# Attention, MoE and MoE on one core: k and v products on two column halves of TensorE, their copies and the norm's small addition on ScalarE

## The chip, the cores and the metric

The kernel runs on one core of a Trainium2 chip. The metric is the device time of one execution in microseconds (us). The engines are called by the profile's names: PE is TensorE (PEld is its weight load), DVE is VectorE, ACT is ScalarE, POOL is GpSimd, SP issues the DMAs.

## The reference

Three layers follow each other. Cut to what matters:

```python
kv = einsum('bhsd,bhse->bhde', k, v)            # 4 batches, 8 heads, 576 tokens, 64 channels, float32
o  = einsum('bhsd,bhde->bhse', q, kv)
x  = o / sqrt(mean(o * o, axis=-1) + 1e-6) * g_norm     # mean over a head's 64 channels
x  = x reshaped to [2304 tokens, 512]
y  = ((x @ w_a) * (x @ w_b)) @ w_out            # weights float64, 512 -> 1536 -> 512
h  = y @ w_in                                   # 512 -> 1024
ln = layernorm(h * softmax(h)) * g_ln
out = ln @ w_out2                               # 1024 -> 512
```

## The kernel before, in words

**Attention.** The 8 heads of a batch are taken as 4 pairs. For a pair, k and v lie beside each other as [128 rows of the sequence, two heads x 64 channels], in four chunks of 128 rows and a tail of 64. `att_kv` (L455) forms k^T v of both heads at once: four matmuls of 128x128 and one of 64x128 for the tail, summed in one PSUM tile `pkv`. Only the two 64x64 blocks on the diagonal are wanted; two DVE copies (L475, L476) put them into `bd`, a 128x128 tile that holds zeros elsewhere. `att_1` (L484) multiplies q by the four `bd` tiles for 128 tokens (the fifth tile of a batch has 64), giving `o` in PSUM. Its norm is a chain through the engines: ACT squares (`sq`, L515) and copies `o` to `x` (L507), DVE sums each head (`r`, L517), DVE multiplies by 1/64 and adds 1e-6 (L519, 8 numbers in a row), POOL raises to the power -1/2 (L521), DVE scales `x` (L522). `att_2` (L527) transposes `x` on PE (`t`, L533) and splits it into `xh` (ACT, L546) and `xl` (DVE, L547). The PSUM tiles pkv, o and t share two slots in turn: a tile waits until the readers of the one two places before it are done.

**Weights.** They come as float64 bits in chunks `raw`; ACT and five DVE instructions (L289 to L307, tiles u and f) decode a chunk, ACT rounds it (L365), POOL makes the low part in two instructions (L366, L367). `w1_0` is the first chunk of feature group 1; `wh` and `wl` are its high and low part.

**The main line.** The first MoE runs over feature groups of 128 and blocks of 384 tokens: `ab` (24 matmuls a block and group, 12 with each of two chunks), and `y` (12). For groups 0 and 1 the six blocks run while attention is still being made; the other groups and the second MoE follow.

**What sets the order.** Every engine takes its instructions in program order. A planner (class `Order`, and the loop from L858) writes that order out, from hand-set durations: PE's order is decided step by step between main line and attention, and the other engines' instructions are placed when their input is expected. So a changed duration or engine in a chain moves instructions on all engines. The planner's price for an `att_kv` block stands at L447, L478 and L852 (1.09).

Of the kernel before, what the change touches and what calls it, by code (L numbers as in the profile page):

```python
# [13 lines left out]
AF = mybir.ActivationFunctionType  # L14
ALU = mybir.AluOpType
AX = mybir.AxisListType

P = 128
# [3 lines left out]
NP = H // 2          # head pairs = k tiles of the model dimension  # L22
# [4 lines left out]
NB = 384             # tokens of a block  # L27
# [3 lines left out]
SC = 4               # whole 128-row chunks of a sequence; the rest is 64 rows  # L31
CH = 512             # columns of a weight chunk

# A float64's upper word, read as a float32, is ordered like its magnitude: from 2^-126 on, where
# the float32s have their full precision, up to the largest value that rounds to a finite float32r.
# [9 lines left out]
class Order:  # L45
    """The order of the instructions: the tensor engine's is decided as it goes, and every other
    engine's operations are issued when what they read is expected to be there."""
# [6 lines left out]
    def chain(self, ops, rank=0, t=None):  # L54
        """Operations (engine, duration, function), each after the one before. Of those that wait
        for an engine the one of the lowest rank goes first, and then the oldest."""
        self.seq += 1
        heapq.heappush(self.events, (self.now if t is None else t, rank, self.seq, 0, list(ops)))

    def until(self, t):  # L60
        """Issue what is due by t."""
# [21 lines left out]
    def wait(self):  # L83
        """Let the next event pass."""
        assert self.events, "nothing left that anything could wait for"
        self.now = max(self.now, self.events[0][0])
        self.until(self.now)

    def load(self, nbytes):
        """A load issued now: when it has arrived."""  # L90
# [4 lines left out]
class Ring:  # L95
    """A rotating buffer's slots: the next one is free once its last user is."""
# [17 lines left out]
def attention_moe_moe_kernel(ctx: ExitStack, tc, kv_in, kv_tail, q_in, g_norm, w1, w_in, w_out2, g_ln, out):  # L114
    """Float32 products are split exactly: hi = the value rounded to float32r (12 bits of
    significand), lo = value - hi (the other 12); hi*hi + hi*lo + lo*hi in three passes.
    The float64 weights come as their bits and become such pairs on the chip."""
# [18 lines left out]
    # Tiles of two banks of PSUM: slot -> when it is free. The attention's two make a fourth.  # L136
# [18 lines left out]
    # ---- constants  # L155
# [20 lines left out]
    # ---- loads: attention's and the weights' chunks ([128, 512] float64s), each kind in its order  # L176
    R_KV, R_TAIL, R_Q, R_RAW = Ring(3), Ring(2), Ring(6), Ring(3)
    arrived = {}                  # what -> (ring slot, tile, when)
# [17 lines left out]
    # Weights between them: so many chunks before the attention's nth load.  # L196
# [4 lines left out]
    def load_one(k):  # L201
# [6 lines left out]
        elif what == "q":  # L208
            r, t, src, n = R_Q, att.tile([P, S], F32, tag="q", name=nm, bufs=6), q_in[x, y], 2304
            if x == 0:  # L210
                # The first block's tokens; the others come later.
# [16 lines left out]
    def loads():  # L228
        """Issue every load whose buffer is free."""
# [21 lines left out]
    # ---- decoding of the weights  # L251
# [10 lines left out]
    def decode_more():  # L262
        """Start on the next chunk, if it is there and the buffers are free."""
# [7 lines left out]
    def rank_of(k):  # L271
        """A chunk's among the attention's tiles: the first ones are wanted soon."""
        return {("w", 0, 0): 1.5, ("w", 0, 1): 1.5, ("w", 0, 2): 2.5, ("w", 1, 0): 2.5}.get(k, 5)

    def decode(k):
# [8 lines left out]
        def a():  # L284
            # |upper word|, on its way to a clamped exponent.
# [10 lines left out]
        def b3():  # L296
            # The float32 of the sign, the exponent and the significand's upper 20 bits.
# [7 lines left out]
        def b5():  # L305
            # The lower 32 bits' value.
# [18 lines left out]
    def store(k, f, u, su, sf, t):  # L325
        """The pair of a chunk, once it has a place."""
# [53 lines left out]
    def wc_used(k):  # L380
        """The last product with a chunk has been issued."""
# [5 lines left out]
    def scale_more():  # L387
        """g_ln goes into the rows of the second MoE's w_out; the first six chunks take the first
        MoE's weights' places, once nothing else wants them."""
# [27 lines left out]
    # ---- attention: the front (k^T v of a pair of heads; q times it for a tile of tokens) and the  # L417
    # back (the transpose of the tile's normalized rows)
# [3 lines left out]
    back = []                      # (ready, b, t, x, ring slot)  # L422
# [21 lines left out]
    def run_front():  # L444
        w, b, i = front.pop(0)
        if w == "kv":
            od.pe(1.09, lambda: att_kv(b, i))  # L447
# [7 lines left out]
    def att_kv(b, p):  # L455
# [3 lines left out]
        o = ps[:, 0:P]  # L459
        for c in range(SC):  # L460
            nc.tensor.matmul(  # L461
                o, lhsT=t[:, c * P:(c + 1) * P], rhs=t[:, (SC + c) * P:(SC + c + 1) * P], start=c == 0, stop=False
            )
        r0 = D * (p % 2)
        nc.tensor.matmul(
            o, lhsT=tl[r0:r0 + D, p // 2, 0:P], rhs=tl[r0:r0 + D, p // 2, P:2 * P], start=False, stop=True
        )
        bd = bds[b % 2, p]

        def done(t):  # L470
# [4 lines left out]
            ("V", 0.13, lambda: nc.vector.tensor_copy(out=bd[0:D, 0:D], in_=ps[0:D, 0:D])),  # L475
            ("V", 0.13, lambda: nc.vector.tensor_copy(out=bd[D:P, D:P], in_=ps[D:P, D:P])),  # L476
            (None, 0, done),
        ], t=od.now + 1.09 + 0.2)  # L478
# [5 lines left out]
    def att_1(b, t):  # L484
        """Attention of 128 (or the last 64) tokens, over the root mean square of each head."""
# [24 lines left out]
        def done(when):  # L510
# [4 lines left out]
            ("A", 0.52, lambda: nc.scalar.activation(out=sq[0:n], in_=o, func=AF.Square)),  # L515
# [3 lines left out]
            ("V", 0.07, lambda: nc.vector.tensor_scalar(  # L519
                out=r[0:n], in0=r[0:n], scalar1=1.0 / D, scalar2=1e-6, op0=ALU.mult, op1=ALU.add)),  # L520
# [472 lines left out]
```

## Time and profile before

| | us |
|---|---|
| runs before | 748.85, 749.93 (median), 753.9 |
| span of the profiled execution | 748.1 |
| PE busy | 726.2 (97%) |
| DVE busy | 483.2 (65%) |
| POOL busy | 281.9 (38%) |
| ACT busy | 237.7 (32%) |

The span runs from the first to the last instruction of the profiled execution; the median run lies 1.8 us above it. Busy shares are means over stages with different limits, so the rows below are read stage by stage. PE records count a float32 matmul twice, since it goes through the array as two records; the main line's float32r matmuls have one record each.

### The profile page before, as it was taken

How to read it: one execution, taken by the hardware profiler on the slowest of the kernel's cores; microseconds unless marked ns; L12 is line 12 of the kernel's file. 1: busy time of each engine (PE TensorE's matmuls, PEld its weight loads, DVE VectorE, ACT ScalarE, POOL GpSimd, SP SyncE). 2: the span in 40 equal slices, each digit the busy share in tenths (PEclk: the TensorE clock that was granted, in tenths of full speed). 3: DMA queues.
4: the chain of work that ended last, by engine and by line, in shares of the span. 5: the costliest groups of instructions: out<-in, count | busy, mean ns of one | idle time of the engine just before them, and what ended most of it. 6: DMA issues, size and time to landing. Idle time of an engine off the chain costs nothing.

```text
span 748.1 us, 10107 instructions
## 1 busy us (share of the span) xinstructions
PE 726.2 (97%) x4024; PEld 680.4 (91%) x4024; DVE 483.2 (65%) x714; ACT 237.7 (32%) x406; POOL 281.9 (38%) x271
## 2 busy tenths in 40 slices
PE   6789999989999999999999999999999999999998
PEld 5668999989999999999999999999878888888887
DVE  4984545489987777777776757566595535546350
ACT  2453435442323232323231313124533222212221
POOL 2774323575746464626262515131421111111110
PEclk9989999999999999999999999999999999999999
DMA  8915230022221212121211110000000000000001
GB/s 291 327 48 172 93 140 1 1 94 76 94 104 50 92 49 93 50 92 47 95 47 67 48 37 29 0 1 1 1 0 29 15 29 28 15 29 14 29 16 55
DMA packets 16334, 46.78 MB, mean 63 GB/s; under 512 B 2080, under 2 KB 3360, under 8 KB 16288
## 3 DMA queue, kind: packets, MB, share of 16 engines
q1 hardware_dynamic: 16288, 46.15, 17.5%
q8 instruction: 31, 0.51, 0.3%
q14 instruction: 15, 0.12, 0.1%
HBM read 41.42 MB, written 4.72 MB: 62 GB/s over the span
## 4 chain that ended last, share of the span: by engine, by line
PE 87%; DVE 8%; issue 1%; DMA 1%; POOL 1%; ACT 1%; SPq 0%; ACTq 0%; POOLq 0%
PE y L643 19%; PE ab L563 12%; PE ab L564 12%; PE ab L565 12%; PE h L565 4%; PE out L565 4%; PE out L564 4%; PE h L563 4%; PE out L563 4%; PE h L564 4%; PE t L792 2%; PE pkv L461 2%; PE o L490 1%; DVE f_w L298 1%; PE t L533 1%
## 5 line engine op out<-in xcount | busy, mean ns | idle before, releaser
L563 PE MATMUL ab<-xh,wh_w 128*128 128x384 f32 x576 | 194.7, 338 | 0.0
L565 PE MATMUL ab<-xh,wl_w 128*128 128x384 f32 x576 | 193.0, 335 | 0.3 <-POOL wl_w L367 0.3
L564 PE MATMUL ab<-xl,wh_w 128*128 128x384 f32 x576 | 192.8, 335 | 0.0
L616 POOL TENSOR_TENSOR gl<-a,gh 128x384 fp32r<-128x384 f32 x72 | 75.8, 1052 | 162.9 <-ACT gh L615 162.9
L656 DVE TENSOR_TENSOR ya<-y,ya 128x768 f32<-128x768 f32 x120 | 111.2, 949 | 6.5 <-PE y L643 5.1
L563 PEld LDWEIGHTS ab<-xh,wh_w 128*128 128x128 f32 x576 | 108.3, 188 | 0.8 <-issue 0.2
L565 PEld LDWEIGHTS ab<-xh,wl_w 128*128 128x128 f32 x576 | 108.4, 188 | 0.6 <-POOL wl_w L367 0.6
L564 PEld LDWEIGHTS ab<-xl,wh_w 128*128 128x128 f32 x576 | 108.4, 188 | 0.0
L643 PE MATMUL y<-gh,wh_w 128*128 128x384 f32 x288 | 98.2, 341 | 1.5 <-ACT gh L615 1.5
L643 PE MATMUL y<-gl,wh_w 128*128 128x384 f32 x288 | 97.3, 338 | 1.4 <-POOL gl L616 1.3
L643 PE MATMUL y<-gh,wl_w 128*128 128x384 f32 x288 | 96.8, 336 | 0.0
L613 DVE TENSOR_TENSOR a<-ab,a 128x384 f32<-128x384 f32 x72 | 39.8, 553 | 80.4 <-ACT a L612 80.2
L366 POOL TENSOR_TENSOR f_w<-f_w,wh_w 128x512 f32<-128x512 f32 x36 | 49.9, 1386 | 64.8 <-ACT wh_w L365 59.6
L612 ACT COPY a<-ab 128x384 f32<-128x384 f32 x72 | 34.4, 478 | 108.5 <-PE ab L565 108.5
L770 DVE TENSOR_REDUCE st<-h 128x1 f32<-128x1024 f32 x18 | 22.0, 1220 | 67.4 <-PE h L565 67.3
L643 PEld LDWEIGHTS y<-gh,wh_w 128*128 128x128 f32 x288 | 54.5, 189 | 2.7 <-ACT gh L615 1.9
L563 PE MATMUL h<-winh,yh 128*128 128x512 f32 x144 | 56.2, 390 | 0.8 <-DVE u L772 0.8
L643 PEld LDWEIGHTS y<-gl,wh_w 128*128 128x128 f32 x288 | 54.6, 190 | 2.2 <-POOL gl L616 2.1
L565 PE MATMUL h<-winh,yl 128*128 128x512 f32 x144 | 56.2, 390 | 0.0
L564 PE MATMUL h<-winl,yh 128*128 128x512 f32 x144 | 56.1, 389 | 0.0
L643 PEld LDWEIGHTS y<-gh,wl_w 128*128 128x128 f32 x288 | 54.6, 190 | 0.0
L615 ACT CAST gh<-a 128x384 fp32r<-128x384 f32 x72 | 36.9, 513 | 47.3 <-DVE a L613 47.1
(92 smaller groups left out, 1168.7 us busy)
## 6 DMA issues: line engine op xcount, KB each, us to landing
raw_w<-in_w SPq DMA_DIRECT2D x36, 512.0 KB, 3.3
kv<-in_kv SPq DMA_DIRECT2D x16, 512.0 KB, 4.8
out<-ot SPq DMA_DIRECT2D x17, 256.0 KB, 2.0
raw_i<-in_w_in SPq DMA_DIRECT2D x8, 512.0 KB, 3.2
raw_o<-in_w_out SPq DMA_DIRECT2D x8, 512.0 KB, 3.2
q<-in_q SPq DMA_DIRECT2D x12, 288.0 KB, 5.6
tail<-in_kv_tail SPq DMA_DIRECT2D x4, 256.0 KB, 5.7
q<-in_q SPq DMA_DIRECT2D x4, 192.0 KB, 4.2
```

What stands on the lines that cost most here:

```text
L366: ("G", 1.23, lambda: nc.gpsimd.tensor_tensor(out=f, in0=f, in1=hi.bitcast(F32), op=ALU.subtract)),
L461: nc.tensor.matmul(o, lhsT=t[:, c * P:(c + 1) * P], rhs=t[:, (SC + c) * P:(SC + c + 1) * P], start=c == 0, stop=False)
L563: nc.tensor.matmul(o, lhsT=ah, rhs=bh, start=first, stop=False)
L564: nc.tensor.matmul(o, lhsT=ah, rhs=bl, start=False, stop=False)
L565: nc.tensor.matmul(o, lhsT=al, rhs=bh, start=False, stop=last)
L612: ("A", 0.41, lambda: nc.scalar.copy(out=a, in_=ps[:, 0, 0:NB])),
L613: ("V", 0.5, lambda: nc.vector.tensor_tensor(out=a, in0=ps[:, 1, 0:NB], in1=a, op=ALU.mult)),
L615: ("A", 0.41, lambda: nc.scalar.copy(out=gh, in_=a)),
L616: ("G", 0.96, lambda: nc.gpsimd.tensor_tensor(out=gl, in0=a, in1=gh.bitcast(F32), op=ALU.subtract)),
L643: nc.tensor.matmul(o, lhsT=x[:, s], rhs=y, start=f == fs[0] and n == 0, stop=f == fs[-1] and n == 2)
L656: op = ("V", 0.87, lambda: nc.vector.tensor_tensor(out=dst, in0=src, in1=dst, op=ALU.add))
L770: ("V", 1.13, lambda: nc.vector.tensor_reduce(out=nmax, in_=ps, axis=AX.XY, op=ALU.max, negate=True)),
```

## The change

The products of a pair are formed head by head: ten matmuls of 64x64 in place of five of 128x128 (the tail included). Head 0 goes to PSUM partitions 0 to 63, head 1 to 64 to 127, so each uses one half of the array's columns, and the two alternate. The two copies to `bd` and the small addition of the norm move from DVE to ACT; the factor 1/64 goes into the square's input scale. The planner's price of an `att_kv` block becomes 0.75, and the ACT copies are planned at 0.25 and the addition at 0.2. Comments are dropped, without effect.

```diff
     def run_front():
...
-            od.pe(1.09, lambda: att_kv(b, i))
+            od.pe(0.75, lambda: att_kv(b, i))
...
     def att_kv(b, p):
...
-        o = ps[:, 0:P]
-        for c in range(SC):
-            nc.tensor.matmul(
-                o, lhsT=t[:, c * P:(c + 1) * P], rhs=t[:, (SC + c) * P:(SC + c + 1) * P], start=c == 0, stop=False
-            )
         r0 = D * (p % 2)
-        nc.tensor.matmul(
-            o, lhsT=tl[r0:r0 + D, p // 2, 0:P], rhs=tl[r0:r0 + D, p // 2, P:2 * P], start=False, stop=True
-        )
+
+        for c in range(SC + 1):
+            for h in range(2):
+                o = ps[h * D:(h + 1) * D, 0:D]
+                if c < SC:
+                    k, v = (t[:, x * P + h * D:x * P + (h + 1) * D] for x in (c, SC + c))
+                else:
+                    k, v = (tl[r0:r0 + D, p // 2, x * P + h * D:x * P + (h + 1) * D] for x in range(2))
+                nc.tensor.matmul(o, lhsT=k, rhs=v, start=c == 0, stop=c == SC)
...
         od.chain([
-            ("V", 0.13, lambda: nc.vector.tensor_copy(out=bd[0:D, 0:D], in_=ps[0:D, 0:D])),
-            ("V", 0.13, lambda: nc.vector.tensor_copy(out=bd[D:P, D:P], in_=ps[D:P, D:P])),
+            ("A", 0.25, lambda: nc.scalar.copy(out=bd[0:D, 0:D], in_=ps[0:D, 0:D])),
+            ("A", 0.25, lambda: nc.scalar.copy(out=bd[D:P, D:P], in_=ps[D:P, 0:D])),
             (None, 0, done),
-        ], t=od.now + 1.09 + 0.2)
+        ], t=od.now + 0.75 + 0.2)
...
-            ("A", 0.52, lambda: nc.scalar.activation(out=sq[0:n], in_=o, func=AF.Square)),
+            ("A", 0.52, lambda: nc.scalar.activation(out=sq[0:n], in_=o, func=AF.Square, scale=D ** -0.5)),
...
-            ("V", 0.07, lambda: nc.vector.tensor_scalar(
-                out=r[0:n], in0=r[0:n], scalar1=1.0 / D, scalar2=1e-6, op0=ALU.mult, op1=ALU.add)),
+            ("A", 0.2, lambda: nc.scalar.activation(out=r[0:n], in_=r[0:n], func=AF.Copy, bias=1e-6)),
...
-                t += 1.32 if w == "t" else 1.09
+                t += 1.32 if w == "t" else 0.75
```

The order changes on all engines at the start, and from batch 3's last `o` on (PE row 456 of 3632 in both) every engine's remaining order is the same in both kernels. Up to that row PE has 324 matmuls of the main line and all 16 `att_kv` blocks in both.

In the names, `r1_3` is batch 1, tile 3; `gl0_0` is group 0, block 0; a last number counts tiles.

POOL where group 1's weights and batch 1's powers are made, before:

```order
L366 TENSOR_TENSOR f_w1_0_353<-f_w1_0_353,wh_w1_0_420 128x512
L616 TENSOR_TENSOR gl0_0_406<-a0_0_404,gh0_0_405 128x384
L367 TENSOR_TENSOR wl_w1_0_421<-f_w1_0_353,u_w1_0_352 128x512
L366 TENSOR_TENSOR f_w1_1_418<-f_w1_1_418,wh_w1_1_456 128x512
L521 TENSOR_TENSOR r1_0_438<-r1_0_438,mhalf_84 128x8
L521 TENSOR_TENSOR r1_1_448<-r1_1_448,mhalf_84 128x8
L521 TENSOR_TENSOR r1_2_473<-r1_2_473,mhalf_84 128x8
L521 TENSOR_TENSOR r1_3_497<-r1_3_497,mhalf_84 128x8
L521 TENSOR_TENSOR r1_4_521<-r1_4_521,mhalf_84 64x8
L367 TENSOR_TENSOR wl_w1_1_457<-f_w1_1_418,u_w1_1_417 128x512
L366 TENSOR_TENSOR f_w1_2_459<-f_w1_2_459,wh_w1_2_560 128x512
```

and now:

```order
L366 TENSOR_TENSOR f_w1_0_353<-f_w1_0_353,wh_w1_0_435 128x512
L367 TENSOR_TENSOR wl_w1_0_436<-f_w1_0_353,u_w1_0_352 128x512
L616 TENSOR_TENSOR gl0_0_448<-a0_0_446,gh0_0_447 128x384
L366 TENSOR_TENSOR f_w1_1_420<-f_w1_1_420,wh_w1_1_486 128x512
L367 TENSOR_TENSOR wl_w1_1_487<-f_w1_1_420,u_w1_1_419 128x512
L521 TENSOR_TENSOR r1_0_481<-r1_0_481,mhalf_84 128x8
L521 TENSOR_TENSOR r1_1_496<-r1_1_496,mhalf_84 128x8
L521 TENSOR_TENSOR r1_2_528<-r1_2_528,mhalf_84 128x8
L521 TENSOR_TENSOR r1_3_544<-r1_3_544,mhalf_84 128x8
L616 TENSOR_TENSOR gl1_0_566<-a1_0_564,gh1_0_565 128x384
L366 TENSOR_TENSOR f_w1_2_485<-f_w1_2_485,wh_w1_2_553 128x512
L367 TENSOR_TENSOR wl_w1_2_554<-f_w1_2_485,u_w1_2_484 128x512
```

The low part of chunk w1_1 moved from behind the five powers of batch 1 to ahead of them, and the fifth power moved behind w1_2.

DVE around the third `xl` of batch 0, on which the first block of the main line waits, before:

```order
L475 COPY bd1_0_94<-pkv1_0_289 64x64
L519 TENSOR_SCALAR r0_3_247<-r0_3_247 128x8
L517 TENSOR_REDUCE r0_4_271<-sq0_4_270 64x8
L476 COPY bd1_0_94<-pkv1_0_289 64x64
L519 TENSOR_SCALAR r0_4_271<-r0_4_271 64x8
L292 TENSOR_SCALAR u_w0_2_190<-u_w0_2_190 128x512
L547 SCALAR_TENSOR_TENSOR xl0_107<-t0_2_311,gn_82,xh0_106 128x4x128
L298 SCALAR_TENSOR_TENSOR f_w0_2_191<-raw_w0_2_146,u_w0_2_190 128x512
L475 COPY bd1_1_96<-pkv1_1_322 64x64
L522 TENSOR_TENSOR x0_3_245<-x0_3_245,r0_3_247 128x512
```

and now:

```order
L522 TENSOR_TENSOR x0_2_249<-x0_2_249,r0_2_251 128x512
L292 TENSOR_SCALAR u_w0_2_218<-u_w0_2_218 128x512
L547 SCALAR_TENSOR_TENSOR xl0_107<-t0_1_294,gn_82,xh0_106 128x4x128
L518 TENSOR_REDUCE r0_4_308<-sq0_4_307 64x8
L298 SCALAR_TENSOR_TENSOR f_w0_2_219<-raw_w0_2_151,u_w0_2_218 128x512
L522 TENSOR_TENSOR x0_3_266<-x0_3_266,r0_3_268 128x512
L547 SCALAR_TENSOR_TENSOR xl0_107<-t0_2_317,gn_82,xh0_106 128x4x128
L303 TENSOR_SCALAR u_w0_2_218<-f_w0_2_219 128x512
L307 SCALAR_TENSOR_TENSOR u_w0_2_218<-raw_w0_2_151,u_w0_2_218 128x512
L289 TENSOR_SCALAR u_w1_0_352<-u_w1_0_352 128x512
```

The copies and L519 are gone, and the scaling of tile 3 (x0_3), which needs the fourth power, now stands ahead of the third `xl`.

PE from the third transpose of batch 0 on, before:

```order
L533 MATMUL t0_2_311<-ident_81,x0_2_230 128x128 x4
L461 MATMUL pkv1_1_322<-kv1_1_184 128x128 x4
L465 MATMUL pkv1_1_322<-tail1_0_173 128x128
L563 MATMUL ab0_0_334<-xh0_106,wh_w0_0_160 128x384
L564 MATMUL ab0_0_334<-xl0_107,wh_w0_0_160 128x384
L565 MATMUL ab0_0_334<-xh0_106,wl_w0_0_161 128x384
L461 MATMUL pkv1_2_340<-kv1_2_198 128x128 x4
L465 MATMUL pkv1_2_340<-tail1_0_173 128x128
```

and now:

```order
L533 MATMUL t0_2_317<-ident_81,x0_2_249 128x128 x4
L468 MATMUL pkv1_0_322<-kv1_0_179 64x64 x8
L468 MATMUL pkv1_0_322<-tail1_0_183 64x64 x2
L563 MATMUL ab0_0_356<-xh0_106,wh_w0_0_166 128x384
L564 MATMUL ab0_0_356<-xl0_107,wh_w0_0_166 128x384
L565 MATMUL ab0_0_356<-xh0_106,wl_w0_0_167 128x384
L533 MATMUL t0_3_361<-ident_81,x0_3_266 128x128 x4
```

A block is eight and two matmuls of 64x64 in place of four and one; the main line now starts behind batch 1's first block (kv1_0) in place of its second, and the fourth transpose comes right behind the first three matmuls.

## Rows read from the trace of the kernel before

**Rows 1.** The page, head: the span.
```profile
span 748.1 us, 10107 instructions
```
**Rows 2.** Busy time of stretches: us, each engine's busy (instructions), PE clock, DMA.
```profile
40.00:60.00 20.00, 15.86 (x98) 13.30 (x98) 18.26 (x34) 9.17 (x17) 17.98 (x12) 0.91 0.32 105
...
16.50:62.30 45.80, 36.47 (x222) 30.82 (x220) 41.36 (x78) 22.55 (x42) 33.90 (x21) 0.93 0.59 208
62.30:131.90 69.60, 69.60 (x448) 66.80 (x447) 32.91 (x67) 30.20 (x53) 22.34 (x17) 1.00 0.23 79
131.90:748.10 616.20, 609.28 (x3305) 573.41 (x3304) 403.39 (x549) 181.82 (x308) 222.11 (x225) 1.00 0.12 43
```
**Rows 3.** PE's waits in 0 to 130: total us, times, longest.
```profile
PE t L533 <- DVE xl L547: 2.6, 5, 1.1
PE t L533 <- DVE r L519: 2.0, 1, 2.0
PE t L533 <- DVE x L522: 2.0, 2, 1.6
```
**Rows 4.** DVE in order of time: start, us, instruction.
```profile
25.54 0.82 DVE L519 TENSOR_SCALAR r<-r 128x8 f32<-128x8 f32 x1
...
32.42 1.14 DVE L289 TENSOR_SCALAR u_w<-u_w 128x512 f32<-128x512 f32 x1
```
**Rows 5.** Instructions on tiles pkv and r: ns min/median/max, first and last start.
```profile
L475 DVE COPY bd<-pkv x16: 203/216/217, 8.2 to 104.6; 64x64 f32<-64x64 f32 x16
L476 DVE COPY bd<-pkv x16: 227/227/229, 8.4 to 104.8; 64x64 f32<-64x64 f32 x16
...
L519 DVE TENSOR_SCALAR r<-r x20: 154/164/833, 17.5 to 133.4; 128x8 f32<-128x8 f32 x16, 64x8 f32<-64x8 f32 x4
L521 POOL TENSOR_TENSOR r<-r,mhalf x20: 1628/1637/2102, 17.8 to 133.6; 128x8 f32<-128x8 f32 x16, 64x8 f32<-64x8 f32 x4
```
**Rows 6.** PE in order of time around two small tiles and one k, v block.
```profile
83.92 1.09 PE L490 MATMUL o<-bd,q 128*64 128x128 f32 x8
...
85.91 0.33 PE L643 MATMUL y<-gh,wl_w 128*128 128x384 f32 x1
86.08 1.05 PE L461 MATMUL pkv<-kv 128*128 128x128 f32 x8
87.07 0.48 PE L465 MATMUL pkv<-tail 64*128 64x128 f32 x2
87.48 0.44 PE L643 MATMUL y<-gh,wh_w 128*128 128x384 f32 x1
87.77 0.34 PE L643 MATMUL y<-gl,wh_w 128*128 128x384 f32 x1
...
93.86 0.27 PE L533 MATMUL t<-ident,x 64*128 64x64 f32 x1
...
93.86 0.46 PE L533 MATMUL t<-ident,x 64*128 64x64 f32 x4
```
**Rows 7.** Two ACT copies from PSUM: busy us, mean ns; and ns min/median/max.
```profile
L612 ACT COPY a<-ab 128x384 f32<-128x384 f32 x72 | 34.4, 478 | 108.5 <-PE ab L565 108.5
...
L507 ACT COPY x<-o x20: 566/581/608, 17.0 to 132.6; 128x512 f32<-128x512 f32 x16, 64x512 f32<-64x512 f32 x4
```
**Rows 8.** POOL in order of time: batch 1's powers and the split behind them.
```profile
46.26 6.73 POOL L521 TENSOR_TENSOR r<-r,mhalf 128x8 f32<-128x8 f32 x4 [0.19 <-DVE r L519]
...
55.37 1.26 POOL L367 TENSOR_TENSOR wl_w<-f_w,u_w 128x512 fp32r<-128x512 f32 x1
```
**Rows 9.** PE in order of time: places of the start, with waits.
```profile
28.78 0.45 PE L563 MATMUL ab<-xh,wh_w 128*128 128x384 f32 x1
...
40.22 2.38 PE L490 MATMUL o<-bd,q 128*128 128x128 f32 x16
...
49.04 0.63 PE L533 MATMUL t<-ident,x 128*128 128x128 f32 x4 [2.03 <-DVE r L519]
...
57.36 0.44 PE L563 MATMUL ab<-xh,wh_w 128*128 128x384 f32 x1
```

## The prediction, made before the changed kernel ran

> **What bounds the kernel now.** I read the span first [rows 1], then the busy time by stretches [rows 2]. The stretches cut the execution in three. From 62.3 to 131.9 PE is busy for all of 69.60 us: there only PE's own work counts, and an instruction taken off DVE is worth nothing. From 131.9 to the end every engine's order is the same in both kernels, with waits of some 7 us that the change doesn't touch; so that part (616.20 us) should only slide. All of the change's effect lies ahead of 131.9: in the start, and in the blocks that lie in the packed stretch.
>
> In the start (16.5 to 62.3) PE has only 36.47 busy us of 45.80, at 0.93 of its clock, while DVE is busy for 41.36, and POOL for 17.98 of the 20 us from 40 to 60 [rows 2]. PE's waits there end with DVE instructions of the norm: transposes wait for `xl` (2.6 us), the sums and additions (2.0) and the scaling (2.0) [rows 3]. Two further things are seen in order of time. The small addition can cost far more than its size: it took 0.82 us at 25.54, where POOL was at work, and a decode step took 1.14 at 32.42 [rows 4] (its usual length is near 0.43). And the main line's second half of the first group-1 block ran only at 57.36 [rows 9], because the low part of its chunk w1_1 was made on POOL at 55.37, behind all five powers of batch 1 [rows 8].
>
> **The change, part by part.**
>
> *DVE loses work.* A pair's copies take 0.216 + 0.227 = 0.44 us, an addition 0.164 [rows 5]. Some six pairs and nine additions lie in the start: 6 x 0.44 + 8 x 0.164 + 0.82 = 4.8 us by their rows, near 4 net since neighbours overlap by some 0.08 each. That is the most the removal can give by itself.
>
> *ACT gets it.* No row shows an ACT copy of 64 numbers. Above it lie 0.478 for 384 and 0.581 for 512 [rows 7]; their slope, (0.581 - 0.478) / 128 = 0.8 ns a number, gives 0.478 - 320 x 0.0008 = 0.22. From below, nothing goes under zero; I take 0.22, and 0.18 for 8 numbers. In the start that is 6 x 0.44 + 9 x 0.18 = 4.3 us on an engine that was busy for 22.55 of 45.80 [rows 2]: it has room, and this is the cover. What it costs is a queue: an addition now waits behind the squares and copies of later tiles, up to one ACT instruction of 0.6, and POOL's power waits behind it. I take 0.3 each time where POOL is waiting.
>
> *PE: the price of a block.* A block of before started at 86.08, its tail at 87.07, the next main-line matmul at 87.48, and the one after at 87.77; two main-line matmuls otherwise stand 0.17 apart (85.91, 86.08) [rows 6]. So the block took 1.40, and 0.29 - 0.17 = 0.12 more for the matmul behind it: 1.52. Its eight records of four chunks stand (1.05 - 0.27) / 7 = 0.111 apart, taking the first record's length as 0.27; ten of them are 1.11. The other 0.41 is the two changes of tile shape, into the 64-row tail and out of it: 0.2 each.
>
> New: twenty records of 64 moving columns. Rows of such records exist: four of the fifth tile's transpose took 0.46, the first 0.27, so (0.46 - 0.27) / 3 = 0.063 each [rows 6]. In a row, one after the other, twenty take 20 x 0.06 = 1.2; shapes change three times (full to half, half to quarter for the tail, back): 0.6; in all 1.8, dearer than before by 0.28. If the two halves run beside each other, 0.6 + 0.6 = 1.2, cheaper by 0.32. Which holds, no row shows: `o` of a fifth tile uses half the columns (83.92), with records (1.09 - 0.27) / 7 = 0.117 apart [rows 6], as slow as at full width. That says only that width costs nothing by itself, and that half the array was idle. It is nearest to the halves running together, so I take a price near that end, 1.3, and keep 1.2 and 1.8 for the range.
>
> The Trainium skill bears on this. "TensorEngine Tiling (Array Packing)", Key Properties, says that tiles operate independently and that different tiles can load weights and multiply in parallel; by it the block would be 1.2, and the sum below smaller by 11 x 0.1 = 1.1 us. No row here shows it.
>
> *The order.* I follow each engine down its new order with the rows' durations, keeping 1 us aside for every pair of POOL splits that DVE runs into, as rows 4 show it. The main line began at 28.78 [rows 9]; now its first block waits for a third `xl` that stands behind the scaling of tile 3 and so behind the fourth power. Powers take 1.64 [rows 5], with one split of 1.26 among them: I get 29.3, half a us later. Before, two transposes then waited for DVE, and batch 1's first `o` came at 40.22 [rows 9]; now four blocks of batch 1 come in turn with the main line, and I get 39.6. Then the order of POOL pays: w1_1's low part is ready near 44.8 in place of 55.37 + 1.26 = 56.6 [rows 8], and batch 1's powers begin there too, 1.5 us ahead of 46.26. The block of group 1 ends near 47.4; before, PE waited 2.03 at 49.04 and took up that block at 57.36 [rows 9]. Through `y` and batch 1's last transpose I come to 59.5 with 72 main-line matmuls issued. Before, the same transpose ended at 62.3 with 54. So the start leads by 2.8 us and by 18 matmuls of 0.1735: 2.8 + 3.1 = 5.9.
>
> *The packed stretch.* Six blocks lie in it (the others of batch 2, and batch 3): 6 x (1.3 - 1.52) = -1.3 us.
>
> *Ahead of the start.* Up to 16.5 the first four blocks wait for loads in part; shorter blocks bring the first `o` forward by perhaps 0.5 (from 0 to 1.4).
>
> **Sum:** 748.1 - 5.9 - 1.3 - 0.5 = 740.4 as a span [rows 1]. The median of the runs lies 1.8 above the span, so 742.2 us, 1.0% under the median.
>
> **The rivals.**
>
> *The halves run in turn (dearer blocks).* For: no row shows them together. Against: the half-width `o`. Each block costs 1.8. The packed stretch then loses 6 x 0.28 = 1.7 in place of winning 1.3. Five blocks lie on the start's path behind the first main-line matmul, each dearer by 0.5; I count 2.5, and nothing ahead of 16.5. Gain 5.9 - 2.5 - 1.7 = 1.7: span 746.4, time 748.2, no change.
>
> *The lead is lost in a new wait.* The additions sit in ACT's queue, and ACT waits in order for PE's `o` and `t`; POOL, with 17.98 busy of 20 [rows 2], may set the pace of the start whatever DVE is spared, or PE falls to the lower clock again after a wait. For: POOL's share, and the fourth power that now stands ahead of the first block. Against: w1_1 is freed from the powers' queue. Then the start gives 0 to 2 us, the packed stretch 1.3: time 746.5 to 748.5.
>
> *Slower: each change of half is paid.* If the second half's weights can't be loaded while the first half multiplies, a change of half costs like a change of shape, 0.2 [rows 6]. A block alternates nine times: 1.8 + 9 x 0.2 = 3.6, or 2.1 dearer than before. The packed stretch loses 6 x 2.1 = 12.6, and the start 5 x 2.3 = 11.5, of which half may fall into waits: the time is 749.9 - 5.9 + 12.6 + 5.8 = 762. It decides from the point where a block costs 1.3 + 7.7 / 11 = 2.0. Against it: at full width the records of a block stand 0.111 apart, so loads for the same rows do overlap there. The Trainium skill has a rule on this side: "TensorE: Matmul & The Clock Gate", Part 3, says a weight load overlaps running matmuls only where the row group differs, and both halves have the same rows; by it the block would be near this price. The rows at 86.08 contradict it in that form.
>
> *Better.* DVE meets POOL less often than I set aside (three of the four us), and blocks cost 1.2: another 4 us, 738.
>
> **How the numbers follow.** About 1% is what a measurement of this kernel tells from no change: 742.4 is that bound below, 757.4 above. Chances: the forecast (740 to 745) 0.50; halves in turn or the lead lost (745 to 751) 0.26; better (under 740) 0.13; slower by alternation 0.11. Of the forecast's own half about 0.34 lies under 742.4, since the sum stands beside that line: faster 0.13 + 0.34 = 0.47; slower by over 1% 0.10, the rest of the last rival; same 0.43. The range goes from 738, the better case, to 751, the upper end of the two middle rivals, and leaves out the alternation and some 0.05 below. The likeliest case's own range is 740 to 745.
>
> **What would show it.** *Blocks:* `pkv` records 0.03 apart and a block near 1.2 to 1.3 in the packed stretch prove the halves; 0.06 and 1.8 the turn; 0.2 the alternation. *Start:* the main line beginning near 29, w1_1's low part made near 44 ahead of batch 1's powers, and PE packed from some 59 on. *ACT:* copies at 0.22 and additions at 0.18; an addition long after its sum would show the queue. *End:* batch 3's last `o` ends near 124 in place of 131.9, and a stretch behind it as long as before, 616 us. The prediction is wrong if that stretch changes although its order doesn't, or if PE waits again between 62 and 124.

## The result and the profile after

| | us |
|---|---|
| the kernel before, measured beside it | 749.93 median (747.59 to 753.9) |
| the changed kernel | 742.4 median (742.16 to 743.38) |
| ratio, with its 95% interval | 0.990 [0.9876, 0.9925] |
| spans of the profiled executions | 748.1 [rows 1] and 740.5 |

The change saves 7.6 us of the span. The head of the page after:

```profile
span 740.5 us, 10433 instructions
...
PE 719.1 (97%) x4184; PEld 670.9 (91%) x4184; DVE 477.2 (64%) x662; ACT 247.2 (33%) x458; POOL 283.1 (38%) x271
```

The busy time by stretches after, cut at the same times as [rows 2] (us, then each engine's busy time with its instructions, the granted PE clock, the DMAs' share and GB/s):

```profile
0.00:138.44 138.44, 124.92 (x961) 112.55 (x961) 76.21 (x120) 72.37 (x162) 66.84 (x53) 0.96 0.40 145
...
16.50:62.30 45.80, 39.62 (x327) 32.46 (x327) 39.30 (x56) 28.61 (x68) 34.93 (x22) 0.89 0.53 193
62.30:131.90 69.60, 69.23 (x504) 65.14 (x503) 31.07 (x48) 34.88 (x77) 24.59 (x18) 1.00 0.24 88
...
138.44:740.50 602.06, 594.21 (x3225) 558.31 (x3224) 401.02 (x543) 174.86 (x296) 216.21 (x219) 1.00 0.12 44
```

The first and the last of these rows are cut at a mark, not at a time. The mark is the start of the 401st matmul of the main line (those with 384 moving columns): by then all of attention is issued in every kernel of this study, so PE has done the same work up to it. The kernel before gets there at 146.11 us, the changed one at 138.44. The same two stretches of the kernel before:

```profile
0.00:146.11 146.11, 131.06 (x800) 120.58 (x801) 83.62 (x172) 62.70 (x110) 67.11 (x53) 0.98 0.39 137
...
146.11:748.10 601.99, 595.13 (x3225) 559.83 (x3224) 399.63 (x543) 174.99 (x296) 214.80 (x219) 1.00 0.13 44
```

Behind the mark both take 602.0 us. So the whole gain, 146.11 - 138.44 = 7.67 us, lies ahead of it, and two columns split it: PE's busy time there fell from 131.06 to 124.92, by **6.14 us**, and what is left, the time in which PE is not busy, from 146.11 - 131.06 = 15.05 to 138.44 - 124.92 = 13.52, by **1.53 us of waiting**. The readings below use this split. It keeps books and names no cause, and busy time is work at the clock that was granted: that was 0.96 up to the mark after and 0.98 before.

A k, v block in the packed stretch after, PE in order of time (start, us, instruction); its counterpart is [rows 6]:

```profile
89.27 0.34 PE L565 MATMUL ab<-xh,wl_w 128*128 128x384 f32 x1
89.54 0.69 PE L468 MATMUL pkv<-kv 128*64 128x64 f32 x16
90.16 0.33 PE L468 MATMUL pkv<-tail 64*64 64x64 f32 x4
90.42 0.44 PE L563 MATMUL ab<-xh,wh_w 128*128 128x384 f32 x1
90.70 0.34 PE L564 MATMUL ab<-xl,wh_w 128*128 128x384 f32 x1
```

Sixteen records take 0.69, the first of them 0.222 (the median of a record, below): they stand (0.69 - 0.222) / 15 = 0.031 apart in the mean, half of the 0.063 that one of 64 columns took in a row [rows 6]. From 89.54 to the next main-line matmul is 0.88; the block starts 0.27 behind the matmul ahead of it in place of 0.17, and the matmul behind it holds the next one back by 0.28 - 0.17 = 0.11. In all 1.09, against 1.52 before: 0.43 less, and 16 blocks at this price make 6.9 us.

The instructions of the small tiles after (ns min/median/max, first and last start), as [rows 5]:

```profile
L468 PE MATMUL pkv<-kv x256: 222/222/369, 5.5 to 98.9; 128*64 128x64 f32 x128
...
L477 ACT COPY bd<-pkv x16: 207/208/208, 7.8 to 99.8; 64x64 f32<-64x64 f32 x16
...
L520 ACT ACTIVATE r<-r x20: 195/208/227, 16.6 to 125.7; 128x8 f32<-128x8 f32 x16, 64x8 f32<-64x8 f32 x4
```

PE's waits after, over the whole execution (total us, times, longest), to be set against [rows 3]:

```profile
PE pkv L468 <- DMA kv<-in_kv: 6.5, 3, 5.5
...
PE t L533 <- DVE xl L547: 2.4, 3, 1.8
PE t L533 <- ACT x L508: 2.3, 2, 1.8
```

The two waits of 2.0 that ended with DVE's addition and scaling are gone. A new one stands there: transposes wait 2.3 for copies of `o` in ACT's queue.

### The profile page after: what moved, and what is told of

Same layout as the page of the kernel before. It is cut to its first block, busy times and chain, and to the rows that moved or that the text cites. A ratio compares the mean times of both kernels' runs of the same rounds, so it can differ in the third digit from the quotient of the medians.

```text
span 740.5 us, 10433 instructions
## 1 busy us (share of the span) xinstructions
PE 719.1 (97%) x4184; PEld 670.9 (91%) x4184; DVE 477.2 (64%) x662; ACT 247.2 (33%) x458; POOL 283.1 (38%) x271
## 4 chain that ended last, share of the span: by engine, by line
PE 87%; DVE 7%; ACT 2%; POOL 2%; issue 2%; DMA 1%; SPq 0%; ACTq 0%; POOLq 0%
PE y L643 18%; PE ab L563 12%; PE ab L564 12%; PE ab L565 12%; PE h L565 4%; PE out L565 4%; PE h L563 4%; PE out L564 4%; PE out L563 4%; PE h L564 4%; PE t L792 2%; PE o L491 2%; PE pkv L468 2%; DMA kv<-in_kv 1%; DVE f_w L298 1%
## 5 line engine op out<-in xcount | busy, mean ns | idle before, releaser
L613 DVE TENSOR_TENSOR a<-ab,a 128x384 f32<-128x384 f32 x72 | 39.8, 553 | 88.2 <-ACT a L612 88.2
L366 POOL TENSOR_TENSOR f_w<-f_w,wh_w 128x512 f32<-128x512 f32 x36 | 50.3, 1396 | 62.3 <-ACT wh_w L365 62.3
```

The lines of the kernel that those rows point to most:

```text
L366: ("G", 1.23, lambda: nc.gpsimd.tensor_tensor(out=f, in0=f, in1=hi.bitcast(F32), op=ALU.subtract)),
L613: ("V", 0.5, lambda: nc.vector.tensor_tensor(out=a, in0=ps[:, 1, 0:NB], in1=a, op=ALU.mult)),
```

## The experiments

All were timed in three rounds beside the kernel before. The table gathers the mark of each, with its row of busy time (time at the mark, PE's busy time up to it, and the rest), since that is what separates them; the rows themselves follow where a reading rests on them. The median is that of all timed runs (the ratios in the text compare them with the kernel before on the same chip at the same time); the other columns are of the one profiled execution. In the four sets of runs the median of the kernel before lay between 749.93 and 750.87, so a difference of 1 us between two variants tells nothing.

| kernel | median us | mark | PE busy | rest |
|---|---|---|---|---|
| before | 749.9 to 750.9 | 146.11 | 131.06 | 15.05 |
| act: copies and addition on ACT only | 750.98 | 145.15 | 130.50 | 14.65 |
| halves: products on halves only, price 0.75 | 749.81 | 145.90 | 125.60 | 20.30 |
| halves_oldprice: the same, price 1.09 | 745.46 | 145.86 | 125.02 | 20.84 |
| halves_copies: halves and copies | 744.68 | 142.32 | 126.87 | 15.45 |
| halves_add: halves and addition | 744.86 | 141.15 | 124.06 | 17.09 |
| after | 742.4 | 138.44 | 124.92 | 13.52 |
| turn: after, heads not alternating | 745.54 | 141.81 | 127.84 | 13.97 |
| w11_late: after, one split later | 744.16 | 140.12 | 123.71 | 16.41 |
| after_oldprice: after, price 1.09 | 746.19 | 142.23 | 124.84 | 17.39 |
| p85: after, price 0.85 | 745.2 | 141.31 | 125.16 | 16.15 |
| p65: after, price 0.65 | 742.53 | 138.94 | 123.50 | 15.44 |

Two theories stood at the start. The first: the lead comes from DVE's relief and from GpSimd's new order, in which w1_1's low part is made ahead of batch 1's powers. The second: it comes from shorter blocks on PE. (In the expectations the first is told apart into two.)

### One part at a time: `halves` and `act`

`halves` takes over the new products and the price 0.75, and leaves copies and addition on DVE:

```diff
-            ("A", 0.25, lambda: nc.scalar.copy(out=bd[0:D, 0:D], in_=ps[0:D, 0:D])),
-            ("A", 0.25, lambda: nc.scalar.copy(out=bd[D:P, D:P], in_=ps[D:P, 0:D])),
+            ("V", 0.13, lambda: nc.vector.tensor_copy(out=bd[0:D, 0:D], in_=ps[0:D, 0:D])),
+            ("V", 0.13, lambda: nc.vector.tensor_copy(out=bd[D:P, D:P], in_=ps[D:P, 0:D])),
...
-            ("A", 0.2, lambda: nc.scalar.activation(out=r[0:n], in_=r[0:n], func=AF.Copy, bias=1e-6)),
+            ("V", 0.07, lambda: nc.vector.tensor_scalar(
+                out=r[0:n], in0=r[0:n], scalar1=1.0 / D, scalar2=1e-6, op0=ALU.mult, op1=ALU.add)),
```

> Only the k, v products on column halves, with the planner's 0.75; copies and addition stay on DVE. Theory 1 (the start's lead comes from POOL making w1_1's low part ahead of batch 1's powers; the packed stretch's gain from blocks at 1.09 in place of 1.52): here the order still puts w1_1 behind the powers, so the start leads by 1 us at most, and 6 to 7 packed blocks give 2.6 to 3.0: a span of 744 to 745. Theory 2 (the work taken off DVE gives the lead): the same here, 744 to 745, since DVE keeps its work. Theory 3 (the shorter blocks give all): 740.5 to 741.5, as with the whole change.

Measured: ratio 0.9984 [0.9968, 1.0001], no gain. `act` is the other half: the kernel before, with copies and addition on ACT and products at full width.

> Only the copies and the addition on ACT; full-width products and the planner's 1.09. POOL's new order has w1_1's low part ahead of the powers here too. Theory 1 and theory 2: the start leads by 4 to 5 us, the packed stretch (blocks at 1.52) gives nothing: span 743 to 744.5. Theory 3: 747.5 to 748.5.

Measured: ratio 1.0004 [0.999, 1.0018], no gain either. Their busy time up to the mark, of halves:

```profile
0.00:145.90 145.90, 125.60 (x961) 113.59 (x962) 83.93 (x172) 62.50 (x110) 66.95 (x53) 0.96 0.39 138
```

and of act:

```profile
0.00:145.15 145.15, 130.50 (x801) 120.09 (x802) 76.46 (x120) 72.00 (x162) 65.69 (x53) 0.98 0.39 138
```

In `halves` PE has 5.46 us less to do than before, and waits 5.25 us more: the saving on PE was turned into waiting, nearly to the last tenth. In `act` DVE has 7.2 us less to do (83.62 to 76.46), and PE's work and rest are nearly as before (0.6 and 0.4 less; this execution, 748.97, was the fastest of its ten). So neither part brought the gain by itself, each in the one order that was run here; `halves_oldprice`, below, changes this for the halves. What PE waits for in `halves` is seen on DVE in order of time (start, us, instruction):

```profile
53.92 0.22 DVE L476 COPY bd<-pkv 64x64 f32<-64x64 f32 x1
54.06 2.86 DVE L523 TENSOR_TENSOR x<-x,r 128x512 f32<-128x512 f32 x1
56.93 0.23 DVE L477 COPY bd<-pkv 64x64 f32<-64x64 f32 x1
```

and on PE there (in brackets the idle time ahead, and what ended it):

```profile
57.22 1.01 PE L534 MATMUL t<-ident,x 128*128 128x128 f32 x4 [4.05 <-DVE bd L477]
```

A scaling that usually takes 0.69 took 2.86 beside GpSimd's splits, and the second copy of a block stood behind it. POOL in order of time there:

```profile
53.89 1.25 POOL L367 TENSOR_TENSOR wl_w<-f_w,u_w 128x512 fp32r<-128x512 f32 x1
55.11 1.26 POOL L366 TENSOR_TENSOR f_w<-f_w,wh_w 128x512 f32<-128x512 f32 x1
```

The transpose needs the PSUM slot that this copy frees, and waited 4.05.

### Two of three parts: `halves_copies` and `halves_add`

`halves_copies` is the changed kernel with the addition back on DVE; `halves_add` has the copies back on DVE instead (the lines above).

> The change without its third part: the products on halves and the copies on ScalarE, the addition back on VectorE. Theory A (VectorE and TensorE hold the start in turn, so the halves pay only as far as VectorE is relieved; the copies carry most of the relief, 12 pairs of 0.44 us by 62 us, 5.3 us of VectorE's time, against some 15 additions of 0.16, 2.5 us): most of the gain stays, span 742 to 744.5, batch 3's last o ends at 125 to 128. Theory B (the gain hangs on the order, on w1_1's low part standing ahead of batch 1's powers, which this kernel does not have): span 746 to 748.5.

> The change without its second part: the products on halves and the addition on ScalarE, the copies back on VectorE. Theory A (VectorE's load; it is relieved of the additions only, about a third of what the change takes from it): span 745 to 747.5, batch 3's last o ends at 128 to 131. Theory B (the order on GpSimd, in which w1_1's low part stands ahead of batch 1's powers, as here): span 741 to 743.5.

Measured: 0.9913 [0.9882, 0.9943] and 0.9917 [0.9893, 0.9941], spans 744.4 and 743.2. Theory B (the order on GpSimd decides) is refuted by the first, which gains with the old order there; theory A's sizes by the second, which gains more than the additions' share (there theory B's 741 to 743.5 held). What the rows show is simpler. Of halves_copies:

```profile
0.00:142.32 142.32, 126.87 (x961) 115.10 (x961) 78.57 (x140) 69.52 (x142) 65.91 (x53) 0.95 0.40 141
```

and of halves_add:

```profile
0.00:141.15 141.15, 124.06 (x960) 112.90 (x961) 82.39 (x152) 65.74 (x130) 66.02 (x53) 0.98 0.40 142
```

Both have PE's saving (4.2 and 7.0 us), and either relief of DVE holds the rest near its old size (15.45 and 17.09 against 20.30 in `halves`). The first also worked at a lower clock (0.95 against 0.98), and its busy time is longer for the same instructions.

### Do the two halves run beside each other? `turn`

The change's loop alternates between the heads, so that neighbouring records use different columns. This kernel does all four chunks of head 0 first, then head 1's:

```diff
-        for c in range(SC + 1):
-            for h in range(2):
+        for c, h in [(c, h) for h in range(2) for c in range(SC)] + [(SC, 0), (SC, 1)]:
+            if True:
```

> The changed kernel with the same 64x64 products in another sequence: four chunks of head 0, then four of head 1, then the two tails, so that neighbours lie on the same half of the columns. If the two halves run beside each other when they alternate, the chunks' records stand 0.06 apart here in place of 0.03, a block costs 16 x 0.03 = 0.5 more, six or seven packed blocks 3 to 3.5 and the start 1 to 2: span 744.5 to 746. If the gain is that only wanted products are made (64 moving columns), nothing changes: 740.5 to 741.5.

Measured: 0.9929 [0.9907, 0.9951], a span of 743.7, 3.2 longer than the changed kernel's and just under the 744.5 to 746 of the first expectation. Its block, PE in order of time:

```profile
91.75 0.97 PE L468 MATMUL pkv<-kv 128*64 128x64 f32 x16
92.64 0.33 PE L468 MATMUL pkv<-tail 64*64 64x64 f32 x4
92.91 0.44 PE L563 MATMUL ab<-xh,wh_w 128*128 128x384 f32 x1
```

The records stand (0.97 - 0.222) / 15 = 0.050 apart in the mean in place of 0.031, and the block takes 0.28 more (0.97 against 0.69). The single starts in the traces tell why. With alternation the records of the two halves start in pairs, 0.007 apart, and the next pair 0.058 later; here the records of one half start 0.058 apart, and pairs are seen only at the seam, where head 1 begins beside head 0's last records. So each half keeps its own pace, and the two work at the same time. Up to the mark PE is busy 127.84 - 124.92 = 2.9 us longer, at a clock of 0.99 against 0.96; the rest is the same (13.97 and 13.52). By these blocks 0.28 of the 0.43 saved, two thirds, hang on the alternation, 16 x 0.28 = 4.5 us in all, and some 3 came out; the other 0.15 comes without it.

### GpSimd's order: `w11_late`

The changed kernel, with w1_1's low part planned 8 us later, behind batch 1's powers, where it stood before:

```diff
+        if k == ("w", 1, 1):
+            def later(when):
+                od.chain([ops[2], (None, 0, done)], rank=rank_of(k) - 0.01, t=when + 8.0)
+
+            od.chain(ops[:2] + [(None, 0, later)], rank=rank_of(k) - 0.01, t=t)
+            return
```

> The changed kernel, but the second POOL instruction for chunk w1_1 is planned 8 us later, so that it stands behind all five powers of batch 1 again, as in the kernel before; DVE keeps its relief and the blocks stay on halves. Theory 1: the half block of group 1 waits again, and 3 to 4 us of the start's lead go: span 743.5 to 744.5. Theory 2: the place of w1_1 matters little, 740.5 to 741.5.

Measured: 0.9919 [0.9897, 0.9941], span 742.2: 1.7 us, between the two. PE's rest rises from 13.52 to 16.41 while its busy time falls by 1.2 (clock 0.98 in place of 0.96). The mechanism is there, and is worth about a quarter of the gain; the intervals of the two ratios overlap, so its size is rough.

### The planner's number: `after_oldprice`, `p85`, `p65`, `halves_oldprice`

The price of a block sets no work, only the order that the planner writes. In the changed kernel it stands at 0.75. These kernels differ from it, or from `halves`, in that number alone (all three places):

```diff
-            od.pe(0.75, lambda: att_kv(b, i))
+            od.pe(1.09, lambda: att_kv(b, i))
```

> The change with the planner's price of a block left at 1.09 in place of 0.75. Theory A (the engines' work and not the planner's number makes the gain): span 740 to 742. Rival (the lower price, which lets the planner put blocks sooner and other engines' work earlier, makes a part of it): span 743 to 746.

> The change with the planner's price of a block at 0.85 in place of 0.75. Theory P (chance of the order): span 740 to 745, anywhere in it. Rival 1 (the price near the measured block, 0.88, makes the plan fit the chip best): span 739 to 740. Rival 2 (a lower price is better): span 741.5 to 743, between 740.5 at 0.75 and 744.3 at 1.09.

> The change with the planner's price of a block at 0.65 in place of 0.75. Theory P (the price only shuffles the order, and each order is worth a few us by chance): span 741 to 745, with no side. Rival (a lower price puts the blocks and what follows from them earlier, and the start gains by it as it did from 1.09 to 0.75): span 739 to 740.5.

> The products on halves alone (copies and addition on VectorE), now with the planner's price of a block left at 1.09. Theory A (alone, the halves are worth nothing because VectorE's copies and additions hold the start, whatever the order): span 746.5 to 748.5. Rival (the halves with price 0.75 fell on a poor order, and shorter blocks are worth about the 0.43 us each that the trace shows, some 12 blocks, in any other): span 742.5 to 745.5.

Measured: 0.9943 [0.9923, 0.9962] at 1.09, 0.9939 [0.9922, 0.9955] at 0.85, 0.9903 [0.9889, 0.9918] at 0.65. With the same instructions, the medians run from 742.4 (0.75) over 742.5 (0.65) and 745.2 (0.85) to 746.2 (1.09). The row of after_oldprice up to the mark:

```profile
0.00:142.23 142.23, 124.84 (x960) 113.29 (x961) 76.33 (x120) 72.22 (x162) 66.23 (x53) 0.96 0.40 141
```

PE's busy time is the changed kernel's to 0.1 us; its rest is 3.9 longer. Three more orders can't tell a rule (0.85, near the 0.88 from a block's start to the next matmul, is not the best, and the lowest is not better than 0.75); they do tell that the order alone is worth 3 to 4 us here.

`halves_oldprice` turned a reading of mine round. With the old price the halves alone give 0.9937 [0.992, 0.9954], 745.46: they are not worth nothing, the order at 0.75 was a poor one for them. With this run four kernels at the price 1.09 form a square, as ratios to the kernel before:

| price 1.09 | copies and addition on DVE | on ACT |
|---|---|---|
| full-width products | 1 | 1.0004 (`act`) |
| products on halves | 0.9937 (`halves_oldprice`) | 0.9943 (`after_oldprice`) |

There the halves give 0.6% (some 4.5 us) with or without the moves to ACT, and the moves give nothing with or without the halves. One price is not one order, since the planner writes each kernel's own; that the two pairs agree to 0.1% speaks against chance and does not exclude it. At 0.75 it is otherwise: the halves alone give nothing clear of noise (0.9984), and with the moves 0.990. So about 3 us of the gain come with the order at 0.75, and in that order the moves are needed.

(The profiled execution of `halves_oldprice`, 749.79, was the longest of ten; the next was 746.97, so its row in the table is not that of its median.) That execution shows where such an order can still lose time, in the packed stretch, PE in order of time:

```profile
101.50 0.44 PE L644 MATMUL y<-gh,wh_w 128*128 128x384 f32 x1 [0.53 <-ACT gh L616]
102.87 0.44 PE L644 MATMUL y<-gl,wh_w 128*128 128x384 f32 x1 [0.92 <-POOL gl L617]
...
104.31 0.52 PE L644 MATMUL y<-gh,wl_w 128*128 128x384 f32 x1
104.63 0.52 PE L644 MATMUL y<-gh,wh_w 128*128 128x384 f32 x1
```

Two waits of 1.45 in all, and some 1.4 us later ten matmuls 0.32 apart in place of 0.17, another 1.5.

### A later stall: `w22_4` and `a15_20`

Both kernels stall where the second feature group ends; after, PE in order of time:

```profile
143.61 0.45 PE L643 MATMUL y<-gh,wh_w 128*128 128x384 f32 x1 [1.54 <-ACT gh L615]
144.72 0.45 PE L643 MATMUL y<-gl,wh_w 128*128 128x384 f32 x1 [0.66 <-POOL gl L616]
```

The product a1_5 (L613) stands on DVE behind the whole decoding of chunk w2_2. `w22_4` plans that decoding 4 us later, `a15_20` plans a1_5's chain 2 us earlier:

```diff
-            rank=rank_of(k), t=max(od.now, when),
+            rank=rank_of(k), t=max(od.now, when) + (4.0 if k == ("w", 2, 2) else 0.0),
```

> The change, with the decoding of one later weight chunk (w2_2) planned 4 us later on VectorE, so that the low part of a1_5 (L613) stands ahead of it. The changed kernel waits there 1.54 us for ScalarE's gh and 0.66 for GpSimd's gl at 143.6 to 144.7. If that queue on VectorE is the cause: the two waits go, and with them the lower clock behind them; span 737 to 739 (740.5 less 2.2 of waits, less up to 1.5 of clock). Rival (the low part waits for what is made ahead of it on ScalarE and GpSimd, whatever VectorE's order): span 740 to 741.5. Also open: that w2_2 then comes late, and the wait stands in front of its first product.

> The change, with one later operation planned earlier: the addition chain of a1_5 starts 2 us sooner, so that its product L613 stands on VectorE ahead of the last step of w2_2's decoding (0.69 us) and its copy gh on ScalarE ahead of an abs. The waits at 143.6 and 144.7 (1.54 and 0.66) shorten by 0.7 and by up to 0.5: span 739 to 740 if the order further on stays as good; as the run that moved w2_2's whole decoding showed (3.4 us gained by 180 us, 16 lost behind it), the rival is that a later chunk's decoding falls behind a product that waits: span above 742.

Measured: 1.0058 [1.0034, 1.0083] and 0.9924 [0.9909, 0.9939], 755.55 and 744.25; both slower than the changed kernel (`a15_20` by 1.9 us, with ratios whose intervals overlap). The first did what was expected where it was expected: its 601st main-line matmul runs at 174.93 in place of 178.32, 3.4 us sooner. The rest is lost further on. There a chunk's decoding now stands on DVE behind a row of products that wait for ACT's copies of PE's `ab`, here one of them (w22_4, DVE in order of time):

```profile
220.99 0.56 DVE L613 TENSOR_TENSOR a<-ab,a 128x384 f32<-128x384 f32 x1 [3.77 <-ACT a L612]
...
222.34 1.14 DVE L289 TENSOR_SCALAR u_i<-u_i 128x512 f32<-128x512 f32 x1
```

Until that chunk is decoded its load buffer isn't free. The waits of the queue of loads there (180 to 240, total us, times, longest):

```profile
SPq L225 <- DVE u_i L307: 33.6, 2, 29.0
```

The loads stood for 29.0 us, and DVE had to catch up behind them; the stretch from 260 to 300 (columns as above), in which the changed kernel's PE is busy throughout:

```profile
260.00:300.00 40.00, 34.56 (x170) 32.60 (x171) 39.45 (x49) 11.69 (x22) 20.27 (x16) 0.91 0.23 79
```

In `a15_20` the first wait shortens as expected, from 1.54 to 0.81, and the 501st matmul comes 1.5 us sooner. Then a new stall stands at the end of the next group, PE in order of time:

```profile
169.28 0.45 PE L643 MATMUL y<-gh,wh_w 128*128 128x384 f32 x1 [1.24 <-ACT gh L615]
170.37 0.53 PE L643 MATMUL y<-gl,wh_w 128*128 128x384 f32 x1 [0.64 <-POOL gl L616]
170.70 0.52 PE L643 MATMUL y<-gh,wl_w 128*128 128x384 f32 x1
```

It waits 1.9 us, and eleven matmuls behind it run 0.32 apart, another 1.6. `a15_20` had been expected at 739 to 740, or above 742 if a later stall came up; `w22_4`, expected at 737 to 741.5, was missed by far. Neither is a version to keep; no kernel of the study was measurably faster than the changed one.

## Why the prediction was right, point by point

It said 742.2, and 742.4 was measured; the span was to be 740.4 and is 740.5. The total is right, and so is its largest term; the two small ones are off, one 0.5 too large and one 0.7 too small. That they nearly cancel, so that the sum agrees to 0.2 us, is luck.

**Ahead of the start: 0.5 predicted, nothing of it lasted.** I took the first blocks to wait for loads. They did so for little (0.28 before, 0.81 after, below); PE was slow there, and a block is dearer. Before, two starts of blocks and the first `o`:

```profile
8.46 2.08 PE L461 MATMUL pkv<-kv 128*128 128x128 f32 x8 [0.28 <-DMA kv<-in_kv]
...
11.20 1.70 PE L461 MATMUL pkv<-kv 128*128 128x128 f32 x8
...
14.75 2.05 PE L490 MATMUL o<-bd,q 128*128 128x128 f32 x16
```

and after:

```profile
8.38 1.12 PE L468 MATMUL pkv<-kv 128*64 128x64 f32 x16 [0.81 <-DMA kv<-in_kv]
...
9.85 1.12 PE L468 MATMUL pkv<-kv 128*64 128x64 f32 x16
...
13.03 4.17 PE L491 MATMUL o<-bd,q 128*128 128x128 f32 x17
```

A block took 11.20 - 8.46 = 2.74 and takes 9.85 - 8.38 = 1.47, and the first `o` starts at 13.03 in place of 14.75, 1.7 us sooner. But the same `o` records run at half the pace now, 17 of them in 4.17 us against 16 in 2.05, and the sixteenth ends at 16.8 in both kernels: the lead is gone. Going by their pace, the changed kernel's records ran at the lower clock up to 16.8, those of the kernel before up to about 12. The granted clock that the profile gives for 0 to 16.5 is 1.00 in both and does not show it; why the full pace came later is not shown.

**The start: 5.9 predicted, 5.7 measured.** The last transpose of batch 1 and the matmul behind it, before:

```profile
61.86 0.46 PE L533 MATMUL t<-ident,x 64*128 64x64 f32 x4
62.25 0.45 PE L643 MATMUL y<-gh,wh_w 128*128 128x384 f32 x1
```

and after:

```profile
59.28 0.46 PE L533 MATMUL t<-ident,x 64*128 64x64 f32 x4
59.67 0.45 PE L563 MATMUL ab<-xh,wh_w 128*128 128x384 f32 x1
```

Counted in the trace, 72 main-line matmuls lie ahead of this place after, as predicted, and 54 before, with ten blocks in both: 62.25 - 59.67 = 2.58, and 18 x 0.1735 = 3.12. The places fell where I put them, against [rows 9]: `o1_0` at 39.57 (39.6), w1_1's low part at 43.68 and batch 1's powers at 44.98 (44.8), the last transpose of batch 1 at 59.28 (59.5); only the main line began sooner, at 28.30 (29.3). POOL in order of time after, against [rows 8]:

```profile
43.68 1.35 POOL L367 TENSOR_TENSOR wl_w<-f_w,u_w 128x512 fp32r<-128x512 f32 x1
44.98 7.01 POOL L521 TENSOR_TENSOR r<-r,mhalf 128x8 f32<-128x8 f32 x4
```

What I had not followed is the clock, 0.89 in 16.5 to 62.3 after and 0.93 before [rows 2], and the queue on ACT (2.3).

**The packed stretch: 1.3 predicted, 2.0 measured** (7.67 at the mark less 5.7). Six blocks lie behind that transpose in both kernels, as I had counted, and each saves 0.43, not 0.22: 2.6, of which 0.3 was waited away (PE is idle for 0.37 from 59.67 to the mark, and for 0.05 in the kernel before). The price of a block, 1.3, was the term that was mis-sized: 1.09 lies below the lower end that I had drawn at 1.2. The records of the two halves do run together (20 x 0.031 = 0.62, as my lower end had it), and the three changes of tile shape take (1.09 - 0.62) / 3 = 0.16 each, where I put 0.2. I had leaned away from the lower end without a row for it.

**The causes.** Here the working misled. I gave the start's lead to DVE's relief (near 4 us) and GpSimd's order, and to the blocks only some 2 us in all. The square at the price 1.09 speaks for the opposite: there the blocks give some 4.5 us and the relief nothing. The other 3 us come with the order at 0.75. In that order the relief is needed: without it PE's saving was waited away (`halves`). What in that order makes the 3 us is shown in part only: `w11_late` puts GpSimd's order at 1.7. Why did the sum come out all the same? I had walked this very order with the rows' durations, and a walk holds what an attribution gets wrong: the shorter blocks and the order were both in it. On ACT a copy took 0.207 and an addition 0.208, where I had 0.22 and 0.18.

**The rivals.** *Halves in turn* is out: records 0.031 apart. `turn` comes near it, with eight records in a row on one half, and costs 3.2 us. *Slower by alternation* is out too. The Trainium skill's rule in "TensorE: Matmul & The Clock Gate", Part 3, that a weight load overlaps running matmuls only where the row group differs, does not hold here: both heads' records use the same 128 rows, by the trace a weight load begins at 89.594 while the records begun at 89.541 and 89.547 still run, and the records overlap best when they alternate between the column halves (0.031 against 0.050). "TensorEngine Tiling (Array Packing)", Key Properties, by which tiles load and multiply in parallel, agrees with these rows. *The lead lost in a new wait* was real in kind (ACT's queue, 2.3 us; two new waits of 0.39 and 0.92 at 155.6 and 157.0), while the clock there was 1.00 after and 0.97 before, so that the two came out even. The same stretch of time before, and then after:

```profile
131.90:200.00 68.10, 65.20 (x362) 63.74 (x362) 54.30 (x73) 26.18 (x47) 41.12 (x32) 0.97 0.19 66
...
131.90:200.00 68.10, 64.29 (x365) 62.81 (x364) 60.78 (x76) 25.82 (x47) 45.98 (x34) 1.00 0.22 78
```

**The end** slid as said: 602.0 us behind the mark in both. Batch 3's last `o` starts its run at 123.20 and ends near 124.3, as predicted (124), and PE was busy for 69.23 of the 69.60 us from 62.3 to 131.9.

**What stays open.** How much of the 7.6 us is this order's luck. Seven kernels here, the changed one among them, have the same instructions and differ in their order alone: six lie between 742.4 and 746.2, one (`w22_4`) at 755.55, and no rule that I tried foretold which would be best. Nor were the kernel before and `act` timed in more orders than one, so what the same work would be worth between the best orders of both is not known.

## What to carry to other kernels

Split a gain at a mark where both kernels have done the same work, into the bound engine's busy time and its waiting. That says where the time went, not why: `halves` lost nearly as much of TensorE's busy time as the whole change (5.5 of 6.1 us) and gained nothing. To find the cause, cross the parts at one setting of everything else: at the old price that told in four kernels that the short blocks give some 4.5 us and the moves off VectorE nothing, where `halves`, run at the new price only, had told that the blocks give nothing. And where a planner writes the order, a number of it that changes no work moved the time by 3 to 4 us, near half the effect that was to be measured: vary it before crediting a part, and expect a local repair (two here) to move a stall on, not to remove it.

## What the runs showed of the hardware that I had not expected

Two 64-column halves of the array, fed alternately from the same rows, take a record every 0.031 us in the mean: each half one in 0.058, both at the same time. A full-width record of 128 columns takes 0.111 [rows 6]. An ACT copy of 64x64 from PSUM takes 0.207 us and a 128x8 addition 0.208, with 64 and with 8 numbers in a row. A DVE scaling of 0.69 took 2.86 while GpSimd ran its splits, four times as long. And waits of 1.45 and 1.9 us on PE cost nearly as much again behind them, when the granted clock fell (ten matmuls 0.32 apart in place of 0.17, at 104 to 107 in `halves_oldprice`; eleven in `a15_20`); the waits of 2.2 at 143.6 in the changed kernel were not followed by that (1.00 in 131.9 to 200), while the same two waits of 1.54 and 0.66 in the kernel before, at 151.28 and 152.39, were (0.97).
